# Attention beside a gated MLP on one core: down products in half-row tiles, and P times V in one run per gate pair

## The chip, the core and the metric

The kernel runs on one core of a Trainium2 chip. A core has TensorE (PE, matrix products into the eight banks of PSUM), VectorE (DVE), ScalarE (ACT), GpSimd (POOL) and SyncE (SP, which here issues most DMAs). Each engine works through its own instructions in order; semaphores order engines against each other. The metric is device time in microseconds (us), lower is better. Times before the change: median 2678.49 us of 3 runs (2673.9 to 2678.52).

## The reference

For x of 2048 rows and 576 columns, with xn its layer norm:

```python
qkv = (xn @ wqkv) -> q, k, v of 32 heads, 18 columns each
p   = softmax(q @ k.T * 18 ** -0.5)          # 2048 x 2048 for each head
s   = concat(p @ v) @ wo
h   = gelu(xn @ w_gate) * (xn @ w_up)        # 4608 columns, tanh form of gelu
out = x + s * silu(h @ w_down)
```

All inputs and the output are fp32.

## The kernel before

**Numbers.** Matrix factors are split into two fp16 parts, a high and a low one, and a product is three fp16 products (high x high, high x low, low x high). Only P times V runs in fp32.

**Stages.** First come the layer norm, the transposes and the projections of the first heads; then V, beside the first pass over the scores of head pair 0. The main loop follows: `for p in range(NPAIR)` over 16 pairs of heads, and in each 64 steps (`i`), one for each block of 512 queries and 128 keys. The last pair (p = 15) also carries the output projection. What comes after it is a short tail.

**A step of the main loop.** It makes one block of scores for the exponentials, `qk2` (L1159): two products of 56 rows, one for each head, side by side in the two 64-row halves of the array, into the two banks `s2`. ScalarE turns them into a tile P of 128 x 1024 fp32 (L1169; two instructions where the heads of the pair belong to different projections). It makes one block of scores of the next pair, `qk1` (L1116), in the same tiling into the two banks `s1`; VectorE reduces that block to row maxima (L1124), which the next pair's exponentials need. A `Deferred` planner (L42) then emits due work of the other engines: `subtick(room)` advances its clock by one and emits entries whose cost fits the room given for ScalarE (A) and VectorE (V). At step 60 `max_end` turns the maxima, on TensorE and with ScalarE's DMAs, into two rows of the next pair's Q.

**The rest of TensorE's work is spread over the steps in cycles of three.** In two steps a part of a *gate pair* runs (`Pair`, L387; `g_run`, L904), in the third P times V and down products.

- A gate pair is a product of xn with 128 columns of w_gate and 128 of w_up for 512 rows of x (or, for 16 of the 160 pairs, of two projections). Its contraction is cut into half-row tiles of 64: in stage 0 the upper array half adds into bank `ma` and the lower into `mb`, in stage 1 the other way round, so that both halves run at the same time and never write one bank. A stage has 14 or 13 slots of two products. Before stage 1 the loop waits until a score bank has been used again (`seen`, `gs.end`). At its end, `gu` (L567) copies `ma` to gs on ScalarE at once, `mb` to gv in the next tick, and makes the gelu in further ticks: a cubic on GpSimd (L590 to L593), tanh on ScalarE, products on GpSimd, and the split into hhi and hlo. When both 128-column parts of a 256-column chunk are done, eight down products go into the queue `dnq`.
- `down(tag)` (L634) is one of them: 128 rows of x, 288 columns, six products over the whole array of 128 rows, into one of the banks `ma`, `mb`, `mc`; then one VectorE pass adds the scaled result to y (L655). Up to four run one after another when no gate pair is open.
- `pv(p, qh, kt, pa, pb)` (L1177) is one unit of P times V: four tiles of 32 array columns, two heads times two query blocks, in fp32, added up in the bank `pv` over the 16 key blocks. After the sixteenth, `norm` (L1192) copies the bank to SBUF on ScalarE (osb, L1198) and divides by the row sums by way of DMAs. There are 512 units in all. The six P buffers hold three units.

**PSUM.** s1 and s2 take two banks each; ma, mb, mc and pv one each.

**Weights** of the next chunk are loaded, reduced to a common scale (L212, L217) and split on ScalarE and GpSimd by a queue `bg` that `subtick` draws from.

Of the kernel before, what the change touches and what calls it, by code (L numbers as in the profile page):

```python
# [96 lines left out]
def kernel(ctx: ExitStack, tc: tile.TileContext, x, wqkv, wo, w_gate, w_up, w_down, out):  # L97
# [10 lines left out]

    defer = Deferred()
# [35 lines left out]
    class MTile:  # L145


        def __init__(self, tag, shape, dt, readers):
            until(lambda: m_pend.get(tag, 0) == 0)
            m_pend[tag] = readers  # L150
            self.tag = tag
            self.t = ps.tile(shape, dt, tag=tag, name=f"{tag}_t")
# [6 lines left out]
    ident32 = ap.tile([P, 512], F32, tag="osb", name="ident32", bufs=1)[:, 0:P]  # L159
# [13 lines left out]
    def prep(name, parts, n, down=None, urgent=False, free=None, dfree=None, lead=1, slow=1):  # L173
# [47 lines left out]
        def small(nm):  # L221
            return ps.tile([P, 512], F32, tag="pv", name=nm)
# [163 lines left out]

    class Pair:  # L387
# [23 lines left out]
        def slot(self):  # L411

            for o, terms in self.q:
                lw, xx = terms[self.k]
                nc.tensor.matmul(  # L415
                    o, lw, xx, start=self.stage == 0 and self.k == 0,
                    stop=self.stage == 1 and self.k == self.slots - 1, skip_group_check=True,
                )
# [111 lines left out]
    def unit_v(w):  # L530
        nc.vector.tensor_copy(EV, w.E[:, 0:1])
        for st in range(NT):
            sl = slice(P * st, P * st + P)
            vst = cp.tile([P, NPAIR, 2, 19], F32, tag=("xo", "sg")[st % 2], name=f"vst{st}", bufs=2)
# [26 lines left out]
        done_units[0] += 1  # L561
# [3 lines left out]
    hstate = {}  # L565

    def gu(w, c, sb, ft):  # L567

        st = {}
        gp = nc.gpsimd  # L570

        def end(g, u):
            st["g"] = wp.tile([P, 512], F32, tag="gs", name=f"gs_{c}_{sb}_{ft}", bufs=1)
            nc.scalar.activation(st["g"], g.t, AF.Copy, scale=w.uE[:, 0:1])  # L574
            g.done()
            defer.at(defer.now + 1, lambda: up(u), on_act())
# [3 lines left out]
        def up(u):  # L580
            st["v"] = wp.tile([P, 512], F32, tag="gv", name=f"gv_{c}_{sb}_{ft}")
# [3 lines left out]
            defer.at(defer.now + 3, th, on_act())  # L585

        def cubic():
            defer.spend(on_pool(4.2))
# [11 lines left out]
        def hp():  # L600
            defer.spend(on_pool(1.9))
# [18 lines left out]
        def hlo():  # L620
            hs = hstate[c, sb]
# [41 lines left out]

    def unit_c(w, c):
# [10 lines left out]
    def queue_gate(sb):  # L675

        for st in range(4 * sb, 4 * sb + 4):
            def e1(st=st):
                t = sgt[st] = cp.tile([P, D], F32, tag="sg", name=f"sg{st}", bufs=2)
# [34 lines left out]
    def load_wod():  # L714

        wod.raw = cp.tile([P, D], F32, tag="xo", name="wod_raw", bufs=2)
# [50 lines left out]
    def unit_out(qc, whole):  # L767
# [13 lines left out]
        for si in range(2):  # L781
            st = 2 * qc + si
            sl = slice(P * si, P * si + P)
            xo = cp.tile([P, D], F32, tag="xo", name=f"xo{st}", bufs=2)
            nc.sync.dma_start(xo, x[P * st:P * st + P, :])
            if whole:
                ob = cp.tile([P, D], F32, tag="sg", name=f"ob{st}", bufs=2)
            else:
                ob = OB(st)
# [103 lines left out]
    gs.pair, gs.open, gs.end, gs.n, gs.over = None, False, 0, 0, False  # L893


    pe_now, seen, s_use = [0], [0], {}

    def use(tag):
        pe_now[0] += 1
        seen[0] = max(seen[0], s_use.get(tag, 0))  # L900
        s_use[tag] = pe_now[0]
        return tag

    def g_run(n, new=True):  # L904


        while n > 0 and not gs.over:
            if not gs.open:
                if gs.pair is not None and seen[0] <= gs.end:
                    return  # L910
                if gs.pair is None:
                    if not new:
                        return
# [6 lines left out]
            n -= 1  # L920
            if gs.pair.slot():
                gs.open = False
                gs.n += 1
                pe_now[0] += 1
                gs.end = pe_now[0]
                if gs.pair.stage == 2:
                    gs.pair = None

# [199 lines left out]
    def max_end(p):  # L1128
# [12 lines left out]
        def b():  # L1141
            mt = MTile("mc", [P, 1024], F16, 0)
# [15 lines left out]

    def qk2(p, qb, kt, tag):  # L1159
# [6 lines left out]
        pt = ap.tile([P, 2, 512], F32, tag="P", name=f"P_{p}_{qb}_{kt}", bufs=6)  # L1166
# [10 lines left out]
    def pv(p, qh, kt, pa, pb):  # L1177
        if kt == 0:
            ob[0] = ps.tile([P, 512], F32, tag="pv", name=f"pv_{p}_{qh}")
# [11 lines left out]

    def norm(p, qh, o):  # L1192
# [3 lines left out]
        def a():  # L1196
            st["o"] = ap.tile([P, 512], F32, tag="osb", name=f"osb_{p}_{qh}", bufs=1)
# [29 lines left out]
        def d():  # L1227
            if last and qh == 1:
                st["h"] = wp.tile([P, 512], F16, tag="evh", name=f"onh_{p}_{qh}", bufs=3)
            else:  # L1230
                st["h"] = ap.tile([P, 512], F16, tag="onh", name=f"onh_{p}_{qh}", bufs=1)
            nc.scalar.activation(st["h"], st["o"], AF.Copy)

        def e():
            if last and qh == 1:
                st["l"] = wp.tile([P, 512], F16, tag="evl", name=f"onl_{p}_{qh}", bufs=3)
            else:
                st["l"] = ap.tile([P, 512], F16, tag="onl", name=f"onl_{p}_{qh}", bufs=1)
# [60 lines left out]
    load_v(0)  # L1299
    steps = max_end(0)  # L1300
# [18 lines left out]
    G_ALL = 2 * (NB * (NJ - 1) + NCH * NB * 2)  # L1319
    G_SPAN = 4 * NT * (NPAIR - 1) + 8  # L1320
    g0 = gs.n
    nphase = 0
    out_on = False

    for p in range(NPAIR):
        if p not in VT:
            load_v(p)
        for i in range(4 * NT):
            s, half = divmod(i, 2)
            qh, kt = divmod(s, NT)  # L1330
            phase = nphase
            nxt = p + 1 < NPAIR
# [7 lines left out]
            if not (nxt or out_on or dnq) and gs.over and dndone[-1] == NT and ohl_here:  # L1340
                out_on = True
                filler[0] = last_gen()
                left[0] = T_LAST

            pt = qk2(p, 2 * qh + half, kt, "s2" if nxt else ("s1", "s2")[i % 2])
# [6 lines left out]
            if i == 62 and nxt:  # L1352
                steps[2]()
            if out_on:
                subtick()
                fill(left[0] / (4 * NT - i))
            swap = i == 60 and nxt
            if phase >= 2:
                todo, tiles = [], ()
                nphase = 0  # L1360
                if phase == 2:
                    todo = pend[:len(pend) - half]
                    n = next((k + 1 for k, u in enumerate(todo) if u[2] == NT - 1), len(todo))
                    todo, pend = todo[:n], pend[n:]
                if phase == 3:
                    tiles = ("mc", "ma", "mc")
                elif gs.pair is None:
                    tiles = ("mc", "ma", "mb", "mc")
                    if gs.n > g0 + (G_ALL - g0) * (4 * NT * p + i) / G_SPAN:
                        nphase = 3  # L1370
                        tiles = tiles[:1]
                elif len(dnq) > 6:
                    tiles = ("mc",)
                n = min(len(tiles), len(dnq))
                t = 0.6 + 0.86 * len(todo) + 0.75 * n
                if not out_on:
                    subtick(FREE if gs.over else {"A": max(0.75, t - 1.1), "V": 0.75 * (n < 2), "T": t})
                if swap:
                    steps[1]()
                for u in todo:  # L1380
                    pv(*u)
                for tag in tiles:
                    down(tag)
            elif not out_on:
                subtick(FREE if gs.over else SHORT, 3)
                g_run(gs.pair.slots - gs.pair.k if gs.open and phase == 1 else 7)
                nphase = phase + 1
                if swap:
                    steps[1]()
            else:  # L1390
                nphase = phase + 1
            if gs.over:
                down("ma")
                down("mb")
            if gq and (gs.over or phase == 2):
                gq.popleft()()
            if i == 59 and nxt:
                steps = max_end(p + 1)
                steps[0]()
    for _ in filler[0]:  # L1400
# [43 lines left out]
```

## Time and profile before

| | |
|---|---|
| Time, median of 3 runs | 2678.49 us |
| Span of the profiled execution | 2677.8 us |
| Time of the main loop's pairs 0 to 14 in it | 199.8 to 2509.5 us |
| TensorE busy | 2590.3 us |
| VectorE, ScalarE, GpSimd busy | 1858.0, 1666.4, 1490.5 us |

The profile is of one execution of its own, whose span lies 0.7 us below the median of the runs. In its rows, `out<-in` names the tiles, `x` counts the instructions, then come busy us and mean ns of one, then the idle time of the engine just before them and what ended it. `PE` rows are products, `PEld` rows the loads of their weights, which overlap them. Products are pipelined: one of 512 columns has a row of 0.38 us, and the next begins 0.21 us after it began. In the chain of work that ended last each row stands from the end of the row before to its own end.

### The profile page before, as it was taken

The page shows a single profiled execution, that of the slowest core. Times are in us where ns is not written, and L with a number is a line of the kernel's source. Part 1 is how long each engine was busy: PE and PEld are TensorE (multiplying, and loading weights), DVE is VectorE, ACT ScalarE, POOL GpSimd, SP SyncE. Part 2 cuts the span into 40 slices and gives each one's busy share as a digit, 9 for nine tenths or more (in the row PEclk, how much of TensorE's full clock was granted, in tenths as well). Part 3 has the DMA queues.
Part 4 walks back from the last instruction along what each step waited for, and adds up shares of the span by engine and source line. Part 5 has one row for each costly group of instructions (what it writes and reads, how often), then busy time and mean ns, then how long its engine had stood idle before and what let it go on. Part 6 is the DMA issues. An engine that isn't in the chain of part 4 may idle for free.

```text
span 2677.8 us, 52591 instructions
## 1 busy us (share of the span) xinstructions
PE 2590.3 (97%) x21896; PEld 1229.7 (46%) x21896; DVE 1858.0 (69%) x2385; ACT 1666.4 (62%) x2113; POOL 1490.5 (56%) x1422
## 2 busy tenths in 40 slices
PE   6979999999999999999999999999999999999898
PEld 6544444444454444444444444444444444444344
DVE  7686677766776677776767677776767777676444
ACT  5216666666667666666666666667666666666663
POOL 4235655375537555466665757657575666757401
PEclk9999999999999999999999999999999999999999
DMA  4430111302131111111111111111110111100033
GB/s 143 139 94 11 32 41 24 87 13 27 39 96 20 27 36 40 51 32 28 38 39 26 34 28 32 28 38 41 24 44 18 32 28 38 48 9 15 9 101 116
DMA packets 134040, 118.46 MB, mean 44 GB/s; under 512 B 60456, under 2 KB 113088, under 8 KB 133800
## 3 DMA queue, kind: packets, MB, share of 16 engines
q1 hardware_dynamic: 128168, 103.31, 15.0%
q0 software_dynamic: 3072, 8.90, 1.0%
q8 instruction: 171, 2.80, 0.5%
q10 hardware_dynamic: 2560, 2.89, 0.3%
q14 instruction: 69, 0.57, 0.1%
HBM read 85.16 MB, written 29.63 MB: 43 GB/s over the span
## 4 chain that ended last, share of the span: by engine, by line
PE 86%; DVE 7%; ACT 4%; DMA 1%; issue 1%; POOL 0%; SPq 0%; ACTq 0%; DVEq 0%
PE mb_t L415 18%; PE pv L1185 16%; PE ma_t L415 15%; PE mc_t L648 9%; PE s L1163 9%; PE s L1121 8%; DVE PM L1124 3%; PE ma_t L648 3%; PE mb_t L648 3%; ACT P L1169 2%; PE mc_t L432 1%; DVE y L655 1%; PE mb_t L432 1%; PE ma_t L432 1%; PE pv_t L432 0%
## 5 line engine op out<-in xcount | busy, mean ns | idle before, releaser
L1124 DVE TENSOR_REDUCE PM<-s 128x2 f32<-128x1024 f32 x1024 | 1253.1, 1225 | 417.3 <-PE s L1121 401.6
L1169 ACT ACTIVATE P<-s,etab 128x1024 f32<-128x1024 f32 x896 | 997.0, 1113 | 731.9 <-PE s L1163 723.4
L415 PE MATMUL ma_t<-XHT,whi_c 64*128 64x512 f16 x1440 | 542.1, 376 | 5.0 <-ACT gs L574 2.1
L415 PE MATMUL mb_t<-XHT,whi_c 64*128 64x512 f16 x1440 | 542.2, 377 | 1.7 <-ACT gv L582 1.4
L1185 PE MATMUL pv<-P,VT 128*32 128x512 f32 x4096 | 509.0, 600 | 0.0
L415 PE MATMUL ma_t<-XHT,wlo_c 64*128 64x512 f16 x1296 | 487.3, 376 | 0.0
L415 PE MATMUL ma_t<-XL,whi_c 64*128 64x512 f16 x1152 | 434.0, 377 | 0.0
L415 PE MATMUL mb_t<-XL,whi_c 64*128 64x512 f16 x1152 | 433.8, 377 | 0.0
L415 PE MATMUL mb_t<-XHT,wlo_c 64*128 64x512 f16 x1152 | 433.1, 376 | 0.0
L1163 PE MATMUL s<-QT,KT 56*128 56x512 f16 x2048 | 407.1, 381 | 17.5 <-ACT P L1169 10.0
L1121 PE MATMUL s<-KT,QT 54*128 54x512 f16 x2048 | 406.1, 379 | 14.7 <-DVE PM L1124 10.5
L415 PEld LDWEIGHTS <-whi_c 64*128 64x128 f16 x5184 | 272.9, 94 | 309.3 <-issue 24.6
L602 POOL TENSOR_SCALAR tw<-tw 128x512 f32<-128x512 f32 x144 | 89.4, 621 | 494.6 <-ACT tw L596 494.5
L655 DVE SCALAR_TENSOR_TENSOR y<-mc_t,c_c,y 128x288 f32<-128x288 f32 x320 | 165.4, 517 | 233.6 <-PE mc_t L648 233.1
L648 PEld LDWEIGHTS <-hhi 128*128 128x128 f16 x2304 | 207.4, 98 | 245.7 <-issue 199.9
L623 POOL TENSOR_TENSOR hlo<-gv,hhi 128x512 f16<-128x512 f32 x144 | 170.7, 1185 | 235.6 <-ACT hhi L617 235.4
L1163 PEld LDWEIGHTS <-KT 56*128 56x128 f16 x2048 | 127.0, 93 | 262.5 <-issue 185.2
L590 POOL TENSOR_TENSOR tw<-gs 128x512 f32<-128x512 f32 x144 | 150.1, 1042 | 118.9 <-ACT gs L574 118.9
L415 PEld LDWEIGHTS <-wlo_c 64*128 64x128 f16 x2592 | 141.2, 94 | 148.1 <-issue 1.5
L1185 PEld LDWEIGHTS pv<-P,VT 128*32 128x32 f32 x4096 | 99.4, 108 | 218.0 <-issue 216.5
L648 PE MATMUL mc_t<-dhi_c,hhi 128*128 128x288 f16 x676 | 195.3, 289 | 3.7 <-DVE y L653 0.4
L648 PE MATMUL mc_t<-dhi_c,hlo 128*128 128x288 f16 x676 | 193.2, 286 | 0.0
(245 smaller groups left out, 4233.5 us busy)
## 6 DMA issues: line engine op xcount, KB each, us to landing
draw_c<-in_B_w_down SPq DMA_DIRECT2D x18, 576.0 KB
raw_c<-in_B_w_gate SPq DMA_DIRECT2D x18, 512.0 KB
raw_c<-in_B_w_up SPq DMA_DIRECT2D x18, 512.0 KB
obr<-rd SPq DMA_DIRECT2D x31, 256.0 KB
KT<-KD SPq DMA_DIRECT2D x32, 224.0 KB
QT<-QD SPq DMA_DIRECT2D x32, 216.0 KB
VS<-vst POOLq DMA_DIRECT2D x16, 304.0 KB, 3.7
VT<-VS SPq DMA_DIRECT2D x16, 304.0 KB
```

The costliest lines, as they stand in the source:

```text
L415: nc.tensor.matmul(o, lw, xx, start=self.stage == 0 and self.k == 0, stop=self.stage == 1 and self.k == self.slots - 1, skip_group_check=True,
L432: nc.tensor.matmul(o, xx(t), ww[:, t, i, :], start=(k == 0), stop=False)
L590: gp.tensor_tensor(st["t"], st["g"], st["g"], op=ALU.mult)
L602: gp.tensor_scalar(st["t"], st["t"], 1.0, 1.0, op0=ALU.mult, op1=ALU.add)
L623: gp.tensor_tensor(hs.lo[:, ft], st["v"], hs.hi[:, ft], op=ALU.subtract)
L648: nc.tensor.matmul(mt.t[:, 0:288], a[:, ft, sl], b[:, ft, ms], start=(k == 0), stop=(k == 5))
L655: nc.vector.scalar_tensor_tensor(yy, mt.t[:, 0:288], w.c, yy, op0=ALU.mult, op1=ALU.add)
L1121: nc.tensor.matmul(s1[:, h], QT[p][r, P * qt:P * qt + P], KT[p][r, 512 * kb:512 * kb + 512], start=True, stop=True)
L1124: nc.vector.tensor_reduce(PM[p][:, :, qt, kb:kb + 1], s1, op=ALU.max, axis=AX.X)
L1163: nc.tensor.matmul(s2[:, h], KT[p][r, P * kt:P * kt + P], QT[p][r, 512 * qb:512 * qb + 512], start=True, stop=True)
L1169: nc.scalar.activation(pt, s2, AF.Exp, scale=ETAB[j0])
L1185: nc.tensor.matmul(o[qd:qd + 32, :], VT[p][:, c0:c0 + 32], pt[:, h], start=(kt == 0), stop=(kt == NT - 1), skip_group_check=True,)
```

## The change

**Down products.** A new class `DownPair` takes two entries of the queue, the two column halves of one block of rows. It has two banks, `md`. In stage 0 the upper 64 array rows work on column half 0 and the lower 64 on half 1, in stage 1 they are swapped, six slots of two products each. One stage runs in a step. One VectorE pass over both banks (`evac`) adds the result to y. Between the stages a *touch*, a VectorE copy of one element of each bank, orders stage 1 behind stage 0. Gate pairs get a touch in the same place, in place of the rule on reused score banks.

**P times V.** The units of a gate pair's time wait in `pend`. When a gate pair has closed, the next step runs them one after another, a `burst`, into the bank `ma` (and what belongs to the next query half into `mb`). VectorE copies the burst into the SBUF tile osb, or adds it to it. The bank `pv` and `norm`'s copy on ScalarE are gone from the main loop. If held P tiles reach eight and the gate pair isn't closed, a burst goes to `md`.

**Order.** A step runs scores, then a down stage if there is one, then gate slots, as many as keep the spread even (`stored`, with 0.2158 us a slot and 0.735 a stage), or at least 1.27 us of both together, 1.8 in a step with a down pair's second stage. No down pair starts while six or more P tiles are held, unless a gate pair has just closed. The gelu steps wait for those of the pair before (`glu`).

**Memory.** Eight P buffers: six as before, two in a pool that is open in the main loop only (`Stage`); the small tiles that lay there move to other pools. The last head pair keeps the old loop, with `down` over the whole array and P times V in its own bank.

```diff
-        pt = ap.tile([P, 2, 512], F32, tag="P", name=f"P_{p}_{qb}_{kt}", bufs=6)
+        pt = ptile(p, f"P_{p}_{qb}_{kt}")
...
+    def touch(ap):
+
+        t = sm.tile([1, 2], F32, tag="touch", name="touch", bufs=2)
+        o = t[:, 0:1] if len(ap.shape) == 2 else t.rearrange("p (a b) -> p a b", a=2)
+        nc.vector.tensor_copy(o, ap)
...
+            if self.stage == 0:
+                touch(self.b.t[0:1, 0:1])
             self.stage += 1
             if self.stage == 2:
                 self.end(self.a, self.b)
...
         def end(g, u):
+            until(lambda: glu["cubic"] == k)
...
         def up(u):
+            if glu["low"] < k - 1:
+                defer.at(defer.now + 1, lambda: up(u), on_act())
+                return
...
+    class DownPair:
+        def run(self):
...
+            if self.stage == 0:
+                self.t = MTile("md", [P, 2, 512], F32, 1)
+            k = 0
+            for ft in range(2):
+                for a, b in ((hs.hi, w.dhi), (hs.hi, w.dlo), (hs.lo, w.dhi)):
+                    for half in range(2):
+                        r = slice(64 * half, 64 * half + 64)
+                        hf = half ^ self.stage
+                        nc.tensor.matmul(
+                            self.t.t[:, hf, 0:288], a[r, ft, sl], b[r, ft, 288 * hf:288 * hf + 288],
+                            start=self.stage == 0 and k == 0, stop=self.stage == 1 and k == 5,
+                            skip_group_check=True,
+                        )
+                    k += 1
+            if self.stage == 0:
+                touch(self.t.t[0:1, :, 0:1])
...
+        def evac(self):
...
+                nc.vector.scalar_tensor_tensor(yy, y, w.c, yy, op0=ALU.mult, op1=ALU.add)
...
+    def burst(todo, tag):
+
+        p, qh, k0, _, _ = todo[0]
+        k1 = todo[-1][2]
+        t = MTile(tag, [P, 512], F32, 1)
+        for _, _, kt, pa, pb in todo:
+            for b, pt in enumerate((pa, pb)):
+                for h in range(2):
+                    qd = 64 * b + 32 * h
+                    c0 = 38 * kt + 19 * h
+                    nc.tensor.matmul(
+                        t.t[qd:qd + 32, :], VT[p][:, c0:c0 + 32], pt[:, h],
+                        start=kt == k0, stop=kt == k1, skip_group_check=True,
+                    )
+        if k0 == 0:
+            osum[p, qh] = ap.tile([P, 512], F32, tag="osb", name=f"osb_{p}_{qh}", bufs=2)
+            nc.vector.tensor_copy(osum[p, qh], t.t)
+        else:
+            nc.vector.tensor_tensor(osum[p, qh], t.t, osum[p, qh], op=ALU.add)
+        t.done()
+        if k1 == NT - 1:
+            norm(p, qh, None)
...
+            stored += (gs.left * G_SLOT + dleft * D_STAGE) / max(1, whole - 64 * p - i)
+            late = False
+            spent = 0.0
+            held = 2 * len(pend) + (half == 0)
+            cap = 8 if 64 * p + i < whole - 3 else 6
+            if dn is None and len(dnq) > 1 and not 58 <= i <= 60 and (gs.closed or held < cap - 2):
+                dn = DownPair()
+                dn.run()
+                spent = D_STAGE
+            elif dn is not None:
+                late = dn.run()
+                spent = D_STAGE
+            if spent:
+                dleft -= 1
+            stored -= spent
+            if gs.closed:
+                gs.closed = False
+                if late:
+                    dn.evac()
+                    dn = None
+                k = len(pend)
+                subtick({"A": 2.2, "V": 1.4 if late else 2.2, "T": 1.0 + 0.86 * k})
+                flush(("ma", "mb"))
             else:
+                subtick({"A": 0.75, "V": 0.0 if late else 0.75, "T": 1.85})
+                if late:
+                    dn.evac()
+                    dn = None
+                r = g_left()
+                n = max(stored, (1.8 if late else 1.27) - spent) / G_SLOT
+                if n < r:
+                    n = math.ceil(r / max(1, round(r / max(n, 1.0))))
+                n0 = gs.left
+                g_run(n)
+                stored -= (n0 - gs.left) * G_SLOT
+                if held >= cap and not gs.closed:
+                    subtick({"A": 1.5, "V": 1.5, "T": 3.0})
+                    flush(("md",))
```

More of the change, by code (lines that the diff above doesn't have):

```diff
@@ L107, with __init__, open, close @@
     ps = ctx.enter_context(tc.tile_pool(name="ps", bufs=1, space=PSUM))
+    class Stage:
+        def __init__(self):
+            self.sb = self.pt = None
+        def open(self, name):
+            self.close()
+            self.sb = tc.tile_pool(name=f"sb{name}", bufs=1)
+            self.pt = tc.tile_pool(name=f"pt{name}", bufs=1, space=PSUM)
+            self.s, self.p = self.sb.__enter__(), self.pt.__enter__()
+        def close(self):
+            if self.sb is not None:
+                self.pt.__exit__(None, None, None)
+                self.sb.__exit__(None, None, None)
+                self.sb = None
+    stage = Stage()
+    stage.open("a")
+    ctx.callback(stage.close)
+    own = {"mc", "pv", "md"}
     defer = Deferred()
@@ L565 @@
     hstate = {}
+    glu = dict(n=0, cubic=0, hp=0, low=0)
     def gu(w, c, sb, ft):
@@ L620, in hlo @@
         def hlo():
+            glu["low"] += 1
             hs = hstate[c, sb]
@@ L892, with g_left, g_run @@
     gs = W()
-    gs.pair, gs.open, gs.end, gs.n, gs.over = None, False, 0, 0, False
-    pe_now, seen, s_use = [0], [0], {}
+    gs.pair, gs.open, gs.end, gs.over, gs.closed = None, False, 0, False, False
+    gs.left = 27 * NB * (NJ - 1 + 2 * NCH)
+    blocks = [0]
     def use(tag):
-        pe_now[0] += 1
-        seen[0] = max(seen[0], s_use.get(tag, 0))
-        s_use[tag] = pe_now[0]
-        return tag
-    def g_run(n, new=True):
+        blocks[0] += 1
+        return tag
+    def g_left():
+        if gs.over:
+            return 0
+        return gs.pair.slots - gs.pair.k if gs.open else 14
+    def g_run(n):
         while n > 0 and not gs.over:
             if not gs.open:
-                if gs.pair is not None and seen[0] <= gs.end:
+                if gs.pair is not None and blocks[0] <= gs.end:
                     return
                 if gs.pair is None:
-                    if not new:
-                        return
                     gs.pair = next(gstream, None)
@@ L1299 @@
     load_v(0)
+    stage.open("b")
     steps = max_end(0)
@@ L1318, with flush @@
     pend = []
[L1319 to L1325, printed above, removed]
+    dn = None
+    stored = 0.0
+    gs.closed = False
+    G_SLOT, D_STAGE = 0.2158, 0.735
+    whole = (NPAIR - 1) * 4 * NT
+    dleft = 2 * NCH * NT
+    def flush(tags):
+        for tag in tags:
+            if not pend:
+                return
+            n = next((k + 1 for k, u in enumerate(pend) if u[2] == NT - 1), len(pend))
+            burst(pend[:n], tag)
+            del pend[:n]
+    for p in range(NPAIR - 1):
         if p not in VT:
@@ L1339 @@
                 items = iter(range(64))
[L1340 to L1345, printed above, removed]
+            pt = qk2(p, 2 * qh + half, kt, "s2")
             if half == 0:
@@ L1351 @@
                 qk1(kp, next(items))
-            if i == 62 and nxt:
+            if i == 62:
                 steps[2]()
[L1354 to L1389, printed above, removed]
-            else:
-                nphase = phase + 1
@@ L1398, with last_gen @@
+            if i == 60:
+                steps[1]()
+            if i == 59:
                 steps = max_end(p + 1)
                 steps[0]()
+    assert dn is None
+    flush(("md", "md"))
+    stage.open("c")
+    def last_gen():
+        for qc in range(4, 8):
+            yield from unit_out(qc, False)
+        for qc in range(TAIL_QC):
+            yield from unit_out(qc, True)
+    nphase = 0
+    out_on = False
+    p = NPAIR - 1
+    if p not in VT:
+        load_v(p)
+    for i in range(4 * NT):
+        s, half = divmod(i, 2)
+        qh, kt = divmod(s, NT)
+        phase = nphase
+        if i == 0:
+            until(lambda: mdone.get(p))
+        if not (out_on or dnq) and gs.over and dndone[-1] == NT and ohl_here:
+            out_on = True
+            filler[0] = last_gen()
+            left[0] = T_LAST
+        pt = qk2(p, 2 * qh + half, kt, ("s1", "s2")[i % 2])
+        if half == 0:
+            pa = pt
+        else:
+            pend.append((p, qh, kt, pa, pt))
+        if out_on:
+            subtick()
+            fill(left[0] / (4 * NT - i))
+        if phase >= 2:
+            nphase = 0
+            n = next((k + 1 for k, u in enumerate(pend) if u[2] == NT - 1), len(pend))
+            todo, pend = pend[:n], pend[n:]
+            if not out_on:
+                subtick(FREE)
+            for u in todo:
+                pv(*u)
+            down("mc")
+        else:
+            if not out_on:
+                subtick(FREE)
+            nphase = phase + 1
+        if gs.over:
+            down("ma")
+            down("mb")
+        else:
+            g_run(14)
+        if gq:
+            gq.popleft()()
```

90 lines of the change are left out of this document (59 added, 31 removed).

## The prediction

> **What bounds the kernel now.** I read the page's busy times first, then the clock and the chain that ended last, then one question per stage: the busy time of the main loop, the idle time in front of each group of TensorE rows, and the timeline of a few steps.
>
> ```profile
> PE 2590.3 (97%) x21896; PEld 1229.7 (46%) x21896; DVE 1858.0 (69%) x2385; ACT 1666.4 (62%) x2113; POOL 1490.5 (56%) x1422
> PE 86%; DVE 7%; ACT 4%; DMA 1%; issue 1%; POOL 0%; SPq 0%; ACTq 0%; DVEq 0%
> 199.80:2509.50 2309.70, 2277.81 (x19369) 1042.94 (x19368) 1639.53 (x2025) 1514.05 (x1893) 1391.52 (x1285) 1.00 0.14 34
> ```
>
> The third row is the main loop, head pairs 0 to 14 (960 steps): 2309.7 us, of which TensorE (first number after the comma) is busy 2277.8, VectorE (third) 1639.5, or 71%, at a granted clock of 1.00. That is 2.41 us a step. TensorE's order of work is the bound. What the change can win lies in TensorE's gaps. A busy row here also covers the draining of the array, so the chain, which counts from end to end, prices the gaps better:
>
> ```profile
> 1403.48 0.32 PE s L1163 x2
> 1403.80 0.22 PE s L1121 x2
> 1407.77 0.22 PE s L1121 x2
> 1407.98 1.00 PE pv L1185 x8
> 1408.98 0.84 PE mc_t L648 x6
> 1409.82 0.73 PE ma_t L648 x6
> 1416.80 1.85 PE pv L1185 x16
> 1418.66 0.32 PE s L1163 x2
> ```
>
> Eight P-times-V records are one unit (four column tiles, two records each), sixteen are two. So a unit costs 1.85 - 1.00 = 0.85 us and entering the run 0.15. A down product that follows another costs 0.73, the one that follows P times V 0.84: 0.11 for the entry. The score products that follow either cost 0.32 in place of 0.22: 0.10. These are prices of changing the tiling (64 rows, 32 columns, whole array).
>
> **The change part by part.**
>
> *Fewer changes of tiling.* In the timeline of the main loop I count 303 P-times-V runs (first and last below). Of these 207 are followed by down products, the others by scores; 29 more down runs follow 64-row work directly, which I price like the two entries of a down run, 0.21.
>
> ```profile
> 207.03 1.07 PE L1185 MATMUL pv<-P,VT 128*32 128x512 f32 x8
> 2508.54 1.06 PE L1185 MATMUL pv<-P,VT 128*32 128x512 f32 x8
> ```
>
> Before: 303 x 0.15 + 207 x 0.11 + (207 + 96 + 29) x 0.10 + 29 x 0.11 = 105 us. After, down, gate and scores are all 64-row, and only a burst of P times V changes the tiling, 0.15 + 0.10, once a gate pair. A pair has 27 slots; 4320 slots less some 195 run ahead of the loop (25 steps of 5, five of 14) give 152 pairs: 38 us. Gain 67 us.
>
> *Arithmetic.* A down pair runs two stages of six concurrent half-row products of 288 columns in place of two products of six. If a half-row pair takes the time of one whole-array product, a stage takes the 0.73 of the row above, and 576 stages cost what 576 products did: nothing either way. The ends of the range are 0.73 and the case in which a half's weight load isn't hidden behind that half's running product:
>
> ```profile
> 1404.08 0.37 PE L415 MATMUL mb_t<-XL,whi_c 64*128 64x512 f16 x1
> 1404.08 0.37 PE L415 MATMUL ma_t<-XL,whi_c 64*128 64x512 f16 x1
> 1404.29 0.37 PE L415 MATMUL mb_t<-XHT,wlo_c 64*128 64x512 f16 x1
> 1404.08 0.10 PEld L415 LDWEIGHTS <-wlo_c 64*128 64x128 f16 x2
> ```
>
> In this gate slot the loads of both halves for the next slot start together with the running products, take 0.10 together, and the next products follow 0.21 after the last. So they are hidden and side by side; 0.10 is below 0.73 / 6 = 0.12. I take 0.73, with a margin of only 0.02 us. If the load were not hidden, a stage would be 6 x (0.12 + 0.10) = 1.32, or 340 us more over 576 stages.
>
> The Trainium skill speaks against the change here. Its page "TensorE: Matmul & The Clock Gate" says, in "LDWEIGHTS (loading the stationary operand)", that a load takes its column count over 1.2, whatever the rows, 107 ns for 128 columns, and in "The mechanism" that a load overlaps running matmuls only in another row group. By both a stage would be an estimated 6 x (0.12 + 0.107) = 1.36 us and the kernel some 360 us slower. The load's size agrees with the 0.10 row; the overlap does not, since the loads of both row groups start while both are running. No row shows two halves of 288 columns, so it stays as a rival.
>
> *Waits that go.*
>
> ```profile
> L1163 PE MATMUL s<-QT,KT 56*128 56x512 f16 x1920 | 381.5, 381 | 16.5 <-ACT P L1169 9.0 <-ACT P L1172 3.3 <-DVE PM L1124 2.3
> L648 PE MATMUL mc_t<-dhi_c,hhi 128*128 128x288 f16 x676 | 195.3, 289 | 3.7 <-DVE y L653 0.4 <-DVE y L655 0.2
> ```
>
> The score products wait 12.3 us for the exponentials: a step with one P-times-V unit and no down product is shorter than an exponential. With bursts of three units that ends. Down runs lose 3.7 more; with pipelining half hidden in busy time I round the two to 17 us.
>
> *New waits at the end of a gate pair.* The burst is written to ma, the gate product's own bank, and waits for ScalarE's copy gs of that product. P times V had a bank of its own before.
>
> ```profile
> 1406.89 0.38 PE L415 MATMUL ma_t<-XHT,whi_c 64*128 64x512 f16 x1
> 1406.87 0.62 ACT L617 ACTIVATE hhi<-gv 128x512 f16<-128x512 f32 x1
> 1407.39 0.68 ACT L574 ACTIVATE gs<-ma_t,uE_c 128x512 f32<-128x512 f32 x1
> ```
>
> The last gate slot starts at 1406.89 and gs ends at 1408.07, 1.18 later. The burst would be ready after that slot (0.22), two scores (0.22 each) and part of the entry (0.10), 0.76 later: it waits 0.42, and I take 0.45 with the release. A down stage of 0.73 in that step hides the wait; a step without one is bare. Behind the burst VectorE adds ma into SBUF, and the next gate pair begins in ma. The nearest row is a VectorE pass over such a bank and as much SBUF:
>
> ```profile
> L464 DVE SCALAR_TENSOR_TENSOR evl<-ma_t,evh 126x512 f16<-126x512 f32 (+1 forms) x18 | 12.4, 689 | 9.0 <-ACT evh L459 8.7
> L836 DVE SCALAR_TENSOR_TENSOR ft<-fo,EO,y 128x576 f32<-128x576 f32 x8 | 6.4, 810 | 0.9 <-PE fo L752 0.9
> ```
>
> 0.69 and 0.11 of two releases is 0.80 after the burst's end. TensorE would start the gate slot 0.32 + 0.22 - 0.16 (the products' overlap, 0.38 less 0.22) = 0.37 after it: 0.43 of waiting, again hidden by a down stage.
>
> How many ends are bare? Followed by the loop's rules, a gate block of two pairs spans 960 / 152 x 2 = 12.6 steps; its down pairs arrive seven deferred ticks after the second pair's end (up, cubic, tanh, split, subtract, queue) and give eight stages. They cover about one of the two ends, and the rule that starts no down stage from six held P tiles on does not alter that. Walking the 960 steps that way I get 77 bare ends and 72 bare first gate steps: 77 x 0.45 + 72 x 0.43 = 66 us. Sixteen of the pairs are projections, whose first bank is read by ScalarE and then by the 0.69 us VectorE pass: about half of them wait 1 us more, 8 us. At the thirty ends of a query half the burst splits and its second part waits in mb for gv, after gs and one exponential; where the first part has only one unit it costs some 0.7, ten times: 7 us.
>
> *VectorE.* A down pair's result leaves in one pass of 0.81 (the second row above, the same form) for two of 0.52; each down pair and gate pair adds a touch, and each burst an add.
>
> ```profile
> L1124 DVE TENSOR_REDUCE PM<-s 128x2 f32<-128x1024 f32 x1024 | 1253.1, 1225 | 417.3 <-PE s L1121 401.6
> L655 DVE SCALAR_TENSOR_TENSOR y<-mc_t,c_c,y 128x288 f32<-128x288 f32 x320 | 165.4, 517 | 233.6 <-PE mc_t L648 233.1
> L531 DVE COPY EV<-E_v x1: 134/134/134, 52.1 to 52.1; 128x1 f32<-128x1 f32 x1
> L244 DVE TENSOR_REDUCE m_v<-mp_v x1: 272/272/272, 49.8 to 49.8; 1x1 f32<-1x128 f32 x1
> ```
>
> A touch lies between the tiny copy (0.13) and a tiny read of PSUM (0.27); I take 0.16, by the copy. In total VectorE goes from 1640 to 1640 - 288 x 0.23 + 440 x 0.16 + 180 x 0.69 = 1770 us, 77% of the loop: no bound on average. But the second step of a down pair has reduce (starting 0.21 after the scores' last issue), pass and release, 0.21 + 1.26 + 0.81 + 0.09 = 2.37 us, against TensorE's 0.73 + 5 x 0.215 + 0.43 = 2.24. The next down pair's first stage, which needs the same banks, stands 0.1 behind. Some 140 pairs follow directly: 15 us, and with weight reductions that fall into such steps 22. The gate's touch is ready 0.65 after the last slot, when TensorE arrives: nothing, as long as two scores lie between. The bounds of this whole term are 0 and 72 (below).
>
> *At nothing:* two more P buffers (ScalarE waited for P times V 2.3 us in all, below), the osb copy leaving ScalarE, the last head pair, which keeps the old down form, and the shared fp16 buffers of the normalised output, written once in 32 steps.
>
> ```profile
>   ACT P L1169: 2.3, 2
> ```
>
> *Sum* against this execution: -67 - 17 + 66 + 8 + 7 + 22 = +19. Its span of 2677.8 lies 0.7 below the median of the runs, 2678.49, which takes in what lies around the span; 2678 + 19 = 2697 us.
>
> **The rivals.**
>
> *Covered ends (faster).* If the down queue is rarely empty when a gate pair closes, its stage stands ahead of the burst and of the next gate slot, and 66 + 7 us of waiting go: 2624. It decides where the bare ends fall from 77 below some 55, at 0.88 us a bare end against the sum of 19. For it: down work is 576 stages in 960 steps, and the rule gives an open down pair precedence at an end. Against: each block's stages come in one batch, seven ticks late.
>
> *VectorE becomes the bound of the down steps.* Per down pair it needs 2 x 1.26 + 0.81 + 0.19 and about 0.5 of reductions and normalising, 4.02, against TensorE's 4.05. If the small pieces gather there, each pair loses 0.25: 72 us in place of 22, 2747. For it: the reduction's bank s1 is single, so each delay reaches TensorE. Against: in the reductions' row above, VectorE sat idle 402 us waiting for TensorE's scores.
>
> *The 64-row down stage doesn't hold 0.73.* By the loads above +340: 3037 us. The gate rows speak against it.
>
> **How the numbers follow.** What a measurement can tell from no change is 0.2%, 5.4 us. Forecast 0.48, with a range of its own from 2665 to 2730 by the VectorE term's lower end, fewer bare ends and the projections' waits; of it 0.08 faster, 0.07 within 5.4 us, 0.33 slower. Covered ends 0.34 (2590 to 2665), VectorE 0.14 (2730 to 2790), loads 0.04. Faster 0.42, same 0.07, slower 0.51. The range leaves out the lower part of the covered ends and the last few hundredths above: 2622 to 2765.
>
> **What would show it.** Right: P-times-V runs of three or four units, some 150 to 160 in the loop; rows of the half-row down products in pairs 0.12 apart; idle time of TensorE in front of the burst released by gs, and in front of gate products by the burst's add, some 70 times each. Wrong: those idle times missing or under 25 us together (covered ends), idle in front of scores released by the reduction above 40 us (VectorE), or stages of over 0.8 us (loads). If bursts come far more often than 160 times, because held P tiles force them, the first term is wrong.

## The result and the profile after

The changed kernel takes 2700.76 us (median of 4 runs, 2696.62 to 2702.77) against 2678.51 for the kernel before, run beside it: 1.0085 times the time before, 95% interval 1.0071 to 1.0099. The forecast was 2697 us, a ratio of 1.007.

First the busy rows and the chain by engine, from the page of the changed kernel, then three stretches of its profiled execution (up to the first scores of the main loop, the loop of pairs 0 to 14, the rest); the columns are the stretch, its length, and busy us of PE, PEld, DVE, ACT and POOL, then the clock, the DMA share and GB/s.

```profile
PE 2556.7 (95%) x25292; PEld 1359.9 (50%) x25292; DVE 1922.6 (71%) x2718; ACT 1655.4 (61%) x2083; POOL 1485.3 (55%) x1422
PE 76%; DVE 11%; ACT 7%; issue 3%; DMA 2%; POOL 0%; SPq 0%; ACTq 0%; DVEq 0%
0.00:210.00 210.00, 169.11 (x1509) 118.59 (x1510) 147.08 (x245) 66.76 (x130) 74.37 (x112) 0.95 0.41 121
210.00:2542.30 2332.30, 2246.98 (x22795) 1175.17 (x22794) 1707.82 (x2359) 1506.99 (x1869) 1400.91 (x1298) 1.00 0.14 34
2542.30:2699.00 156.70, 140.60 (x992) 66.17 (x988) 67.67 (x114) 81.63 (x85) 10.00 (x12) 0.94 0.30 96
```

TensorE is busy 33.6 us less than before, and yet the kernel is slower: the chain, which was 86% TensorE, is now 76%, and VectorE and ScalarE took its place. That is the shape of switches of the tiling removed and waits added. The loop is 22.6 us longer. The start is 10 us longer and the end 12 us shorter, which is mostly work moved: 53 more gate slots (11 us) run ahead of the loop, where the old rule on reused score banks held them back, and the 40 gate slots that ran after the loop are gone.

Where the loop's time went is seen in the chain of the changed kernel; each row is a start, a length, and what ran.

```profile
1396.77 0.69 ACT gs L608
1397.46 0.04 issue
1397.51 2.83 PE ma_t L1310 x24
1400.33 0.02 issue
1400.35 0.70 DVE osb L1318
1401.05 0.04 issue
1401.10 0.37 PE ma_t L443
...
1403.22 0.74 PE md_t L729 x12
...
1413.47 0.74 PE md_t L729 x12
1414.21 3.57 PE ma_t L1310 x32
1417.78 0.32 PE s L1269 x2
```

The first seven rows are a bare end, a gate pair's end without a down stage in that step. TensorE waits for ScalarE's gs, runs a burst of three units, waits for VectorE's add, and only then starts the next gate pair. The last three rows are a covered end: a down stage of 0.74 us stands ahead of the burst, which follows at once. Rows of the table of waits of the changed kernel (us in total, times, longest) add the bare ends up; `PE` rows are waits of products, `PEld` rows those of the loads of their weights:

```profile
PE ma_t L1310 <- ACT gs L608: 29.3, 71, 1.5
PEld ma_t L1310 <- ACT gs L608: 57.6, 89, 1.8
PE ma_t L443 <- DVE osb L1318: 20.6, 67, 1.7
PE s L1269 <- ACT P L1275: 10.7, 15, 1.9
PE ma_t L1310 <- DVE evl L494: 8.9, 9, 1.2
PE md_t L729 <- DVE touch L413: 4.2, 18, 0.3
PE mb_t L443 <- DVE touch L413: 3.6, 7, 1.8
PE md_t L729 <- DVE y L749: 3.2, 11, 0.3
```

Idle time in these rows begins only when the array has drained. A second count goes from the start of one product to the start of the next in the timeline, takes off what these two kinds of work ordinarily need, and adds up the excess; below this is "by starts". It gives 84 bursts that follow scores directly, with 44.5 us over the ordinary entry of a burst (0.53 each), and 78 gate pairs that follow a burst without a down stage, with 38 us over an ordinary slot (0.49 each).

### The profile page after: what moved, and what is told of

The parts are those of the page before. It is cut to its first block, busy times and chain, and to the rows that moved or that the text cites. A ratio compares the mean times of both kernels' runs of the same rounds, so it can differ in the third digit from the quotient of the medians.

```text
span 2699.0 us, 59766 instructions
## 1 busy us (share of the span) xinstructions
PE 2556.7 (95%) x25292; PEld 1359.9 (50%) x25292; DVE 1922.6 (71%) x2718; ACT 1655.4 (61%) x2083; POOL 1485.3 (55%) x1422
## 4 chain that ended last, share of the span: by engine, by line
PE 76%; DVE 11%; ACT 7%; issue 3%; DMA 2%; POOL 0%; SPq 0%; ACTq 0%; DVEq 0%
PE ma_t L443 15%; PE ma_t L1310 15%; PE md_t L729 13%; PE mb_t L443 13%; PE s L1269 7%; PE s L1217 6%; DVE PM L1220 3%; ACT P L1275 3%; ACT gs L608 2%; DVE osb L1318 2%; DVE y L749 2%; PE pv L1291 1%; PE mc_t L462 1%; PE mb_t L1310 1%; ACT hhi L659 1%
## 5 line engine op out<-in xcount | busy, mean ns | idle before, releaser
L443 PE MATMUL ma_t<-XHT,whi_c 64*128 64x512 f16 x1440 | 541.2, 376 | 22.6 <-DVE osb L1318 18.9
L1310 PE MATMUL ma_t<-P,VT 128*32 128x512 f32 x3624 | 421.6, 597 | 38.7 <-ACT gs L608 29.3
L1269 PE MATMUL s<-QT,KT 56*128 56x512 f16 x2048 | 408.2, 380 | 14.5 <-ACT P L1275 10.7
L443 PEld LDWEIGHTS <-whi_c 64*128 64x128 f16 x5184 | 289.6, 94 | 252.6 <-issue 51.8
L729 PE MATMUL md_t<-dhi_c,hhi 64*128 64x288 f16 x2264 | 340.6, 283 | 7.5 <-DVE touch L413 4.2
L729 PE MATMUL md_t<-dhi_c,hlo 64*128 64x288 f16 x2264 | 340.4, 282 | 0.0
L729 PE MATMUL md_t<-dlo_c,hhi 64*128 64x288 f16 x2264 | 339.9, 282 | 0.0
L729 PEld LDWEIGHTS <-hhi 64*128 64x128 f16 x4528 | 249.4, 94 | 138.9 <-issue 34.7
L1318 DVE TENSOR_TENSOR osb<-ma_t,osb 128x512 f32<-128x512 f32 x142 | 98.0, 690 | 209.3 <-PE ma_t L1310 209.3
L1310 PEld LDWEIGHTS ma_t<-P,VT 128*32 128x32 f32 x3624 | 103.1, 109 | 261.8 <-issue 190.7
```

The source lines that it names most:

```text
L443: nc.tensor.matmul(o, lw, xx, start=self.stage == 0 and self.k == 0, stop=self.stage == 1 and self.k == self.slots - 1, skip_group_check=True,
L729: nc.tensor.matmul(self.t.t[:, hf, 0:288], a[r, ft, sl], b[r, ft, 288 * hf:288 * hf + 288], start=self.stage == 0 and k == 0, stop=self.st ...
L1269: nc.tensor.matmul(s2[:, h], KT[p][r, P * kt:P * kt + P], QT[p][r, 512 * qb:512 * qb + 512], start=True, stop=True)
L1310: nc.tensor.matmul(t.t[qd:qd + 32, :], VT[p][:, c0:c0 + 32], pt[:, h], start=kt == k0, stop=kt == k1, skip_group_check=True,)
L1318: nc.vector.tensor_tensor(osum[p, qh], t.t, osum[p, qh], op=ALU.add)
```

## The experiments

### The burst in idle banks at bare ends

```diff
-                flush(("ma", "mb"))
+                flush(("ma", "mb") if spent else ("md", "ma"))
```

No down products use the two banks of the down pair where the end is bare (VectorE's pass over them may still run). Nothing else moves.

> Edit: at a gate pair's end without a down stage in that step, the burst goes to the two idle banks of the down pair in place of the gate's own bank; the second part of a split burst goes to ma. Theory (bare ends): the changed kernel's waits of the burst for gs (29 us idle in 71 places) and of the next gate pair for the burst's add (21 us idle in 67 places), some 80 us by start times, go for the most part: 2620 to 2645 us. Rival (those waits only stand where ScalarE or VectorE is late anyway, and come back in front of scores, touches or down stages): 2680 to 2705 us, with as much idle time of TensorE under other names.

Measured: 2640.61 us, 0.9854 times the time before (0.9837 to 0.9871). In the waits of this kernel the burst's products wait for gs in one place for 71, their loads in 15 for 89. No row is left in which the gate pair waits for the add; the copy of a first burst (L1316) is waited for in five places, 2.6 us:

```profile
PE ma_t L1310 <- ACT gs L608: 1.1, 1, 1.1
PEld ma_t L1310 <- ACT gs L608: 4.8, 15, 1.4
PE md_t L729 <- DVE touch L413: 4.6, 19, 0.3
PE s L1217 <- DVE PM L1220: 3.9, 11, 0.6
PE md_t L729 <- DVE y L749: 2.6, 9, 0.3
PE s L1269 <- ACT P L1275: 11.2, 16, 1.9
```

The other waits grew little: scores for the exponentials 11.2 us after 10.7, down products for touch and pass as before. By starts some 74 of the 82 us at the bare ends are gone, and some 13 come back elsewhere, 6 of them in front of the transposes of `max_end`, which share the banks `md`. The kernel is 60 us faster than the changed one. So most of the bare ends' waits were TensorE's own loss, and this version beats both kernels.

### All ends bare

```diff
-            if dn is None and len(dnq) > 1 and not 58 <= i <= 60 and (gs.closed or held < cap - 2):
+            if gs.closed:
+                pass
+            elif dn is None and len(dnq) > 1 and not 58 <= i <= 60 and held < cap - 1:
```

> Edit: no down stage runs in a step that begins with a closed gate pair (a started down pair waits a step; down pairs may start with up to six held P tiles so that they keep up). So all ends are bare: 155 in place of the changed kernel's 84, while the first gate steps behind the bursts stay bare as often as before, about 80. Theory (each bare end costs about 0.5 us, whoever stands there): 71 x 0.53 = 38 us more than the changed kernel, 2725 to 2750 us, and twice the idle time released by gs. Rival (a down stage moved out of the end shortens another wait, so that only the sum of work counts): within 10 us of the changed kernel, 2690 to 2711 us.

Measured: 2733.75 us, ratio 1.0205 (1.0188 to 1.0222), 33 us more than the changed kernel. In its waits:

```profile
PE ma_t L1310 <- ACT gs L608: 54.5, 137, 1.1
PE ma_t L443 <- DVE osb L1318: 18.7, 56, 1.0
```

Twice the places and nearly twice the time; the second wait hardly changes (20.6 us in 67 places before the edit). By starts 154 bursts now follow scores directly, and the excess in front of bursts is 34 us more, as much as the whole difference. Together with the run before, the price of a bare end is shown from both sides, and the cover is what a down stage is worth there.

### Down stages over the whole array

```diff
-                    for half in range(2):
-                        r = slice(64 * half, 64 * half + 64)
-                        hf = half ^ self.stage
...
+                    hf = self.stage
+                    nc.tensor.matmul(
+                        self.t.t[:, hf, 0:288], a[:, ft, sl], b[:, ft, 288 * hf:288 * hf + 288],
+                        start=k == 0, stop=k == 5,
+                    )
...
-                touch(self.t.t[0:1, :, 0:1])
+                touch(self.t.t[0:1, 0, 0:1])
```

The second stage now writes the other bank alone, so the touch, which reads the first bank only, no longer orders the two stages; here the edit does more than its expectation says. In the changed kernel the second stages of down pairs lose nothing by starts (all 18 us of waiting stand in front of first stages), so this can't have moved the time by much.

> Edit: each down stage is six products over the whole array for one column half in place of twelve half-row products; everything else, the order, the banks, the touch and the single pass included, as in the changed kernel. Theory (the tiling's price is the entry and exit): 576 stages x (0.11 + 0.10) = 121 us more, less some 10 us where a stage stood next to a wait: 2800 to 2830 us. Rival (half-row stages are themselves slower than whole-array ones, so most of the switches' saving was lost in them): 2700 to 2760 us.

Measured: 2788.35 us, ratio 1.0409 (1.0393 to 1.0425), 88 us over the changed kernel: nearer to the theory than to the rival, but below the theory's range. The chain of this kernel at a down stage:

```profile
1400.23 0.22 PE s L1214 x2
1400.45 0.84 PE md_t L727 x6
1401.29 0.32 PE ma_t L443
...
1401.61 0.21 PE ma_t L443
```

Entry and exit are 0.11 and 0.10 in the chain (0.84 - 0.73, 0.32 - 0.22), as before the change. By starts they are 0.095 each, 101 us for 566 entries and 495 exits into gate slots. What I left out of the expectation is that the entry is no loss where the stage waited anyway: the excess in front of down stages net of the entry falls from 19 to 7 us, which leaves the 88 us. The half-row stage takes 0.74 us in the chain further up, six whole-array products 0.73: the change's saving on switches is real, and nothing was lost in the products.

### Touches issued twice

```diff
         nc.vector.tensor_copy(o, ap)
+        nc.vector.tensor_copy(o, ap)
```

> Edit: each touch is issued twice, 443 more VectorE copies of 0.14 us, 62 us of VectorE. Theory (VectorE is 77% busy and holds TensorE only in down pairs that follow directly): 5 to 25 us more, 2705 to 2725. Rival (VectorE bounds the down steps): nearly all of it, 50 to 62 us more, 2750 to 2765.

Measured: 2718.72 us, ratio 1.0148 (1.0131 to 1.0166), 18 us more for 62 us of VectorE work. VectorE has room for most of it. Where it has not is shown by the waits of a gate pair's second stage for the second copy (3.6 us in 7 places for the single copy of the changed kernel):

```profile
PE mb_t L444 <- DVE touch L414: 7.0, 16, 2.1
PE md_t L730 <- DVE touch L413: 4.6, 20, 0.3
```

By starts the excess in front of gate slots rises from 38 to 50 us, that in front of down stages by 2.

### Six P buffers

```diff
-        if p < NPAIR - 1 and n < 64 * (NPAIR - 1) - 8 and n % 8 >= 6:
+        if False:
...
-            cap = 8 if 64 * p + i < whole - 3 else 6
+            cap = 6
...
-            if dn is None and len(dnq) > 1 and not 58 <= i <= 60 and (gs.closed or held < cap - 2):
+            if dn is None and len(dnq) > 1 and not 58 <= i <= 60 and (gs.closed or held < cap - 1):
```

> Edit: six P buffers in place of eight; a burst is forced at six held tiles and a down pair may start with up to four held (with three, the down products fall behind for good). Theory (the two buffers only space the bursts; the price is 0.25 us for each forced burst plus its waits): a few tens of forced bursts, 2700 to 2740 us. Rival (the eight buffers carry the change, since exponentials wait for P without them): over 2760 us, with ScalarE waiting for P times V.

Measured: 2718.32 us, ratio 1.0151 (1.013 to 1.0172), 18 us more than the changed kernel. The time is the theory's, the mechanism the rival's: there are 167 bursts in place of 155, which at 0.25 us are 3 us, but in the waits of this kernel the exponentials wait for a burst to free a P tile, and its granted clock is lower in places:

```profile
ACT P L1275 <- PE ma_t L1310: 174.2, 119, 1.9
482.60:489.40 6.80, 5.72 (x28) 2.34 (x29) 3.54 (x5) 1.74 (x2) 0.00 (x0) 0.50 0.57 185
```

The wait for P was 2.3 us with six buffers before the change. Part of it is hidden: by starts, waits inside bursts come to 34 us, 11 of them in or beside the slow stretches named below, while only 31 bursts follow scores directly, since the lower limit leads to more covered ends. The second row (columns as in the three stretches above) is a stretch behind a TensorE pause of 5.1 us: the granted clock is 0.50 in it, and gate slots start 0.43 apart in place of 0.21. This trace has nine such stretches in its loop, 44 us together, and the changed kernel's has one, of 7 us; the mean clocks are 0.986 and 0.992. At half the clock 37 us more are worth up to 19 us, as much as the whole difference. So the 18 us are waits and slower clock together, and how they divide is not shown. How the two would stand with the same limit was not tried.

### Three attempts on the waits in front of down stages

Some 18 us remain in front of down stages, in 57 places, with the burst in idle banks or without. In most of them the step before has a second stage and is cut short by the end of a gate stage, and VectorE's pass of 0.81 us with the gate's touch behind it is still under way, as here in the chain of the changed kernel:

```profile
1405.29 1.23 DVE PM L1220
1406.52 0.63 DVE y L749
1407.15 0.01 issue
1407.16 0.14 DVE touch L413
1407.31 0.90 PE md_t L729 x12
```

All three attempts start from the kernel with idle banks.

```diff
-                n = max(stored, (1.8 if late else 1.27) - spent) / G_SLOT
+                n = max(stored, (2.02 if late else 1.27) - spent) / G_SLOT
```

> Edit: the kernel with bare ends in the down pair's banks, and in steps with a second down stage at least 2.02 us of down and gate work in place of 1.8, one gate slot more. Theory (in down pairs that follow directly TensorE waits for VectorE's single pass, some 18 us in 57 places by start times): half or more of it goes, 2625 to 2637 us. Rival (the work moved into these steps is missing elsewhere, where it hid an exponential or a reduction): 2638 to 2655 us.

Measured: 2648.86 us, ratio 0.9887 (0.9872 to 0.9902), 8 us more than without the edit. The excess in front of down stages did not fall (20 us), since a step cut short by a stage's end isn't lengthened by a higher target, and that in front of gate slots rose from 7.5 to 17.6, behind the touch: 62 gate stages waited for it by starts, 16 without the edit.

```diff
-                if late:
-                    dn.evac()
-                    dn = None
                 r = g_left()
...
                 g_run(n)
                 stored -= (n0 - gs.left) * G_SLOT
+                if late:
+                    dn.evac()
+                    dn = None
+                    short = spent + (n0 - gs.left) * G_SLOT < 1.7
...
+            wait, short = short, False
-            if dn is None and len(dnq) > 1 and not 58 <= i <= 60 and (gs.closed or held < cap - 2):
+            if dn is None and not wait and len(dnq) > 1 and not 58 <= i <= 60 and (gs.closed or held < cap - 2):
```

> Edit: the kernel with bare ends in the down pair's banks; in a step with a second down stage the pass over the down banks is issued behind the gate slots and their touch, and after such a step of under 1.7 us of down and gate work no new down pair starts. Theory (the 18 us in front of down stages come from steps cut short by a gate stage's end, so that the next down pair comes before VectorE's pass of 0.81 us is over): most of it goes, 2622 to 2633 us. Rival (VectorE is simply late in these steps; then the waits come back in front of the next gate stage or the scores): 2636 to 2650 us.

Measured: 2674.73 us, ratio 0.9987 (0.9977 to 0.9996), 34 us more than without the edit. Neither the theory nor the rival holds: a touch waits in VectorE's order for the end of a gate stage, and now the pass, and all who need the down banks, wait behind it. In its waits:

```profile
DVE touch L413 <- PE mb_t L443: 104.1, 120, 3.3
PE md_t L729 <- DVE y L749: 20.1, 38, 0.5
PE md_t L1310 <- DVE y L749: 11.2, 29, 1.9
```

The touch's idle time was 40.9 us in the kernel it starts from. The third attempt moves the pass, and keeps the next down pair back, in short steps alone (`short` worked out ahead of the slots as `late and spent + min(n, r) * G_SLOT < 1.7`).

> Edit: as the run before (pass behind the touch, no new down pair in the next step), but only in steps in which the end of a gate stage leaves less than 1.7 us of down and gate work; in all others the pass stands ahead of the gate slots again. Theory (the run before lost because the touch, in front of the pass in VectorE's order, held the pass back in the long steps; in the short ones it is ready almost at once): 2622 to 2636 us, idle time in front of down products for VectorE's pass under 5 us. Rival (any pass behind a touch is late for what follows): 2642 to 2675 us.

Measured: 2646.54 us, ratio 0.9884 (0.9867 to 0.99), 28 us of the 34 back, so the touch in the long steps was what cost. It is still 6 us over the kernel without either edit, little more than the noise of the two runs. Down products no longer wait for the pass, but the burst in the down banks does, as in the run before, and down products wait for the burst's add; now in this kernel:

```profile
PE md_t L1310 <- DVE y L749: 11.2, 29, 1.9
PE md_t L729 <- DVE osb L1318: 7.9, 29, 0.3
```

By starts the excess in front of down stages is 18 us as before, now nearly all for the add, and 100 bursts follow scores directly in place of 84, presumably since no down pair may start behind a short step. One way to lengthen the steps and two to move the pass only moved the wait. Whether it can go without a third pair of banks stays open.

## Why the prediction was right, point by point

- **Fewer changes of tiling, -67.** Confirmed in kind and nearly in size. There are 155 bursts for some 152 forecast (162 gate slots ran ahead of the loop, not 195), and entry and exit cost what the chain gave: 3.57 us for four units is 4 x 0.855 + 0.15. From start to start the switches take 34 us for 94 before, 60 less.
- **Arithmetic, 0.** Confirmed: 0.74 for 0.73 us a stage, and the whole-array run above. In the changed kernel's timeline half-row pairs start 0.12 to 0.13 apart:

```profile
1413.29 0.30 PE L729 MATMUL md_t<-dhi_c,hhi 64*128 64x288 f16 x2
1413.42 0.30 PE L729 MATMUL md_t<-dlo_c,hhi 64*128 64x288 f16 x2
1413.54 0.30 PE L729 MATMUL md_t<-dhi_c,hlo 64*128 64x288 f16 x2
1413.42 0.11 PEld L729 LDWEIGHTS <-hlo 64*128 64x128 f16 x2
```

  The load rule weighed against it, from the section "The mechanism" of "TensorE: Matmul & The Clock Gate" in the Trainium skill, does not hold here: with 288 columns too, the two loads for the next pair start at 1413.42 with the running products of both halves and take 0.11 us together. The same section of the Trainium skill also lets a load into a background weight buffer be pulled ahead of running products, which the prediction left out. Rows of the kernel before already spoke against that rival: its down products over all rows start 0.12 apart, at 1402.71 and 1402.83, with loads of 0.10 to 0.11 beginning at the same times.
- **Waits that go, -17.** Mis-sized. Scores waited for the exponentials 10.0 us in 15 places before and 10.7 in 15 after. The short P-times-V steps are gone, but steps that end with gate slots now meet a late exponential: by starts, and counting the longer waits alone, some 30 places and 11 us where 4 and 3 had been.
- **New waits at a gate pair's end, +66 + 8 + 7.** Confirmed by place, count and price: 84 and 78 bare places for 77 and 72, and 82.5 us by starts for the 74 of the first two terms, the projections' included (evl, 8.9 us idle for 8). The third term, the second part of a split burst, was put too high: by starts it costs 1 us, in two places, for 7 in ten. The run with idle banks takes most of the waits out, the run with all ends bare adds to them.
- **VectorE, +22.** About right in size, 19 us in front of down stages, but not in place: some 60 waits of 0.3 us, where 140 of 0.1 and the weight reductions were forecast. The place was not any pair that follows directly but the step that a gate stage's end cuts short, which the prediction did not name; two thirds of the waits end with the gate's touch. That touch, put at nothing, also holds a gate pair's second stage in 15 places, 6.6 us by starts. The touch takes 0.14 us for 0.16, and VectorE is busy 73% of the loop (1707.8 of 2332.3 us) for 77 forecast. Doubling the touches costs 18 of 62 us, so VectorE isn't the bound.
- **At nothing: two more P buffers.** Right for adding them, but the reason given doesn't hold for taking them away: with bursts this far apart they are worth 18 us, the slower clock included.

The rival of covered ends fell at its own condition: the bare ends did not drop below 55. That 2697 lies within 4 us of the measured time is partly luck. Two gains were put too high, the switches by 7 us and the waits that go by 12. Against that, the waits at the turn of a head pair (the transposes of `max_end` and the steps beside them) fell by 8 us by starts, which the prediction did not have. With these sizes the list comes to some 29 us, or 36 with the gate's touch, and 22 were measured: some 10 us stay unaccounted in this counting. The large terms, switches and bare ends, carry the sign.

## What to carry to other kernels

A bank that two uses share joins their waits: work that moves into a bank still read by another engine needs either that much other work ahead of it or another bank, and a bank whose user is idle just then is free to take. Count the places without cover by the loop's own rules, and price one from the rows; that product decided here, not the sum of the work. And an instruction that only waits still stands in its engine's order: put nothing urgent behind it.

## What was not expected of the hardware

A change of tiling has much the same price wherever it was met: 0.095 us by starts from half rows to the whole array and 0.095 back, and 0.09 to 0.11 into and 0.12 out of the column tiles of the fp32 products. Where the engine would have waited, it costs less or nothing: that is 12 of the 33 us by which the whole-array run (88 us) stayed under the 121 worked out from the chain. The rest is fewer exits than stages and the lower price by starts.
